# Two attention blocks on one core: B's transposed x in 512-token loads, x first on the queues, q and k weights read 128 wide, B's blocks further forward

## Chip, cores, metric

One core of a Trainium2 chip. The metric is device microseconds of one execution, median of several. The profiled span is about 1.8 us below the reported time of the same execution. In the profile's lines PE is TensorE, PEld its weight loads, DVE VectorE, ACT ScalarE, POOL GpSimd and SP SyncE; SPq and ACTq are the queues from which SyncE and ScalarE issue loads. A timeline's line gives the start, the length, the engine and what it does; a bracket is idle time before it and what ended that.

## The reference

Two independent attention blocks on 2048 tokens with 448 channels and 16 heads of 28; their outputs stand side by side.

```python
def _A_ref(x, wq, wk, wv, wo):            # full attention, one k/v head for all 16 q heads
    q = (x @ wq).reshape(B, S, H, Dh) ...  ; k = x @ wk ; v = x @ wv
    p = softmax(einsum(q, k) * Dh ** -0.5) ; o = einsum(p, v)
    return o ... @ wo
def _B_ref(x, wqkv, wo):                  # each token looks at 8 tokens, 2 apart, with 16 k/v heads
    qkv = (x @ wqkv) ...                   # idx = pos - 2 * arange(8), masked below 0
    attn = softmax(where(mask, einsum(q, kg) * scale, -1e9)) ; o = einsum(attn, vg)
    return o ... @ wo
return concatenate([a, b], axis=-1)
```

A needs 16 x 2048 x 2048 exponentials. These are 1024 blocks of 128 x 512.

## The kernel before

The kernel holds a small planner. Each operation has a guessed duration, a rank (`pr`, lower goes first) and an earliest time (`rel`); the planner simulates the engines and fixes each engine's order. On the chip the order is never changed: an engine whose next instruction has to wait stands still, and so does everything behind it.

The exponentials: scores of 3 and 2 blocks in turn go to PSUM, and ScalarE takes 3 or 2 of them in one ACTIVATE. In four rounds of each quad (64 blocks) but the first, VectorE takes one block of the three.

```python
OFF_AT = {q: (0, 2, 5, 7) for q in range(1, 16)}
OFF_AT.update({q: (0, 1, 3, 4, 6, 7, 9, 10) for q in ()})
```

The loads. `xst` is the first quarter of A's x, which TensorE transposes; the rest of x comes by transposing DMA.

```python
a("act", 0.5, ... g.xst <- A_x[0, 0:512] ..., W=["xst"], dsem="i_xa0", land=3.2, pr=-21)
a("act", 1.1, wload(g.wk, ...), W=["wk"], dsem="i_wk", land=3, pr=-20, ninc=2)
a("sp", 1.1, wload(g.wq, g.A_wq, 0, KC), ..., dsem="i_wq0", land=3, pr=-25, ninc=2)
a("gp", 1.5, wload(g.wq, g.A_wq, KC, D), ..., dsem="i_wq", land=4, pr=-7.5, ninc=2)
for c in range(1, NCH):                    # A's second to fourth quarter, 4 x 128 channels each
    for t in range(4):
        a("sp", 1.25, ... transpose=True, W=[("xT", c, t)], land=4.6, pr=-20 + c)
for t in range(4):                         # B's x, all 2048 tokens, 4 x 128 channels
    a("sp", 3.5, ... transpose=True, W=[("xT_B", t)], land=8, pr=0, rel=4)
# [...] wqkv on SP; wqv on GpSimd; output weights, then the zero rows ahead of V, on SP
```

B's q and k, and the ranks of A's v:

```python
g.bank(u.bank, p1=KC), g.wqkv[:, kt, w * D + KC * t:w * D + KC * t + KC],   # KC = 112
pr = c + (0.9 if c else 1.3)               # a_v: v of chunk c, just ahead of k of chunk c + 1
B0 = 30.0                                  # B's first block is planned from here on
```

## Time and profile before

| | before |
|---|---|
| time, median of 3 | 463.41 us (463.3 to 463.55) |
| profiled span | 461.54 us |
| ScalarE busy | 447.3 us (97%) |
| first exponential starts | 10.94 us |
| last exponential starts | 453.95 us |
| waits between exponentials over the floor | 8.84 us |

Recorded ScalarE instructions overlap by about 0.1 us, so a wait shorter than that leaves no idle time. I took the starts of ScalarE's instructions from the trace. By the median, the next one starts 0.904 us behind a 1024-wide ACTIVATE (0.903 at best), 1.330 us behind a 1536-wide one, and 0.306 and 0.054 us behind e_t and gcol, two small helpers on ScalarE. With these the 410 exponentials need 434.17 us from the first start to the last. This sum is called the floor; what the stretch takes beyond it are waits. A wait is given at the start of the ACTIVATE in front of it: the 0.87 us at 23.7 us is the one that ends with the start at 25.49, where the page has 0.65 us of idle time.

### The profile page before, as it was taken

The numbers are of one execution on the slowest core, as the hardware profiler recorded it, in microseconds if no ns is written. First come the engines' busy times: TensorE is split into PE (matmuls) and PEld (weight loads), VectorE is DVE, ScalarE is ACT, GpSimd is POOL, SyncE is SP. The second block draws the span as 40 slices with busy tenths as digits, with TensorE's granted clock in tenths as the row PEclk, the third lists the DMA queues.
The fourth block names the chain that finished last, engine by engine and source line by source line (L and its number), as shares of the span: only waits on it lengthen the run. The fifth ranks groups of instructions, "written<-read, shape, count | busy, mean of one in ns | idle before, by whom it ended". The sixth has DMA issues, their size and how long they took to land.

```text
span 461.5 us, 8681 instructions
## 1 busy us (share of the span) xinstructions
PE 422.8 (92%) x3649; PEld 168.2 (36%) x3701; DVE 365.9 (79%) x607; ACT 447.3 (97%) x430; POOL 9.3 (2%) x28
## 2 busy tenths in 40 slices
PE   7889998999998999999989999999899998997995
PEld 2332332333542434334432443334343442443331
DVE  6447888989899796888888688898889878687853
ACT  3999999999999999999999999999999999999994
POOL 7000000000000000000000000000000000000000
PEclk9999999999999999999999999999999999999999
DMA  8991121000401220002201230002200330410001
GB/s 150 164 229 33 48 75 60 11 0 22 161 21 53 89 74 27 1 14 87 91 11 50 81 101 11 12 0 92 86 26 20 111 101 12 136 46 0 11 3 48
DMA packets 41718, 27.34 MB, mean 59 GB/s; under 512 B 17090, under 2 KB 41520, under 8 KB 41680
## 3 DMA queue, kind: packets, MB, share of 16 engines
q1 hardware_dynamic: 40080, 25.35, 19.5%
q0 software_dynamic: 304, 0.73, 0.9%
q10 hardware_dynamic: 1296, 0.71, 0.5%
q8 instruction: 29, 0.48, 0.4%
q14 instruction: 9, 0.07, 0.0%
HBM read 17.60 MB, written 5.52 MB: 50 GB/s over the span
## 4 chain that ended last, share of the span: by engine, by line
ACT 88%; PE 8%; DVE 1%; DMA 1%; issue 0%; ACTq 0%
ACT expT L800 88%; PE ps L783 2%; PE ps L832 1%; PE ps L958 1%; DMA wk<-in_A_wk_dram 1%; PE ps L973 1%; PE ps L781 1%; PE ps L733 1%; PE ps L1059 1%; ACT e_t L1034 0%; PE ps L662 0%; PE ps L917 0%; DVE kT L679 0%; PE ps L747 0%; DVE PV_T L893 0%
## 5 line engine op out<-in xcount | busy, mean ns | idle before, releaser
L800 ACT ACTIVATE expT<-ps 128x1024 bf16<-128x1024 f32 (+1 forms) x410 | 441.7, 1232 | 2.8 <-PE ps L783 2.4
L783 PE MATMUL ps<-qT,kT 32*128 32x512 bf16 x833 | 123.3, 384 | 16.2 <-ACT expT L800 12.9
L832 PE MATMUL ps<-expT,v_aug 128*32 128x512 bf16 x964 | 96.1, 389 | 0.1
L864 DVE TENSOR_SCALAR d_x<-ps 128x512 f32<-128x512 f32 x60 | 41.5, 691 | 39.0 <-PE ps L783 36.8
L783 PEld LDWEIGHTS ps<-qT,kT 32*128 32x128 bf16 x833 | 30.3, 91 | 94.5 <-ACT expT L800 75.3
L781 PE MATMUL ps<-qT,kz 128*128 128x512 bf16 x160 | 50.2, 382 | 10.7 <-ACT expT L800 8.3
L832 PEld LDWEIGHTS ps<-expT,v_aug 128*32 128x32 bf16 x964 | 24.6, 93 | 60.4 <-issue 57.7
L999 DVE TENSOR_TENSOR stage<-qTB,kTB 112x1024 bf16<-112x1024 bf16 x64 | 42.2, 679 | 2.7 <-PE ps L1008 2.7
L1059 PE MATMUL ps<-ident,prod 128*112 128x128 bf16 x512 | 43.9, 225 | 0.0
L1053 DVE TENSOR_TENSOR prod<-Vsh,a_n 128x896 bf16<-128x896 bf16 x64 | 37.8, 616 | 7.2 <-PE ps L1059 7.2
L958 PE MATMUL ps<-xT_B,wqkv 128*112 128x512 bf16 x128 | 40.5, 398 | 0.1
L1059 PEld LDWEIGHTS ps<-ident,prod 128*112 128x112 bf16 x512 | 34.4, 129 | 16.8 <-issue 14.1
L874 DVE SCALAR_TENSOR_TENSOR d_u<-d_u,d_x 128x1024 f32<-128x1024 f32 x30 | 36.4, 1215 | 0.0
L876 DVE SCALAR_TENSOR_TENSOR dexp<-d_u,d_x 128x1024 int16<-128x1024 f32 x30 | 36.4, 1214 | 0.0
L872 DVE SCALAR_TENSOR_TENSOR d_u<-d_x 128x1024 f32<-128x1024 uint16 x30 | 36.3, 1210 | 0.1
L1008 PEld LDWEIGHTS ps<-ones,stage 112*128 112x128 bf16 x512 | 19.4, 96 | 8.4 <-issue 3.2
L1008 PE MATMUL ps<-ones,stage 112*128 112x4 bf16 x512 | 22.1, 167 | 0.0
L781 PEld LDWEIGHTS ps<-qT,kz 128*128 128x128 bf16 x191 | 11.9, 97 | 25.2 <-ACT expT L800 23.1
L958 PEld LDWEIGHTS ps<-xT_B,wqkv 128*112 128x112 bf16 x128 | 14.1, 128 | 16.4 <-issue 11.1
L733 PE MATMUL ps<-xT_A,wq 128*128 128x512 bf16 x57 | 18.3, 383 | 0.6 <-issue 0.3
L1066 PE MATMUL ps<-wo_B,oT 112*128 112x448 bf16 x64 | 18.1, 356 | 0.2 <-DVE oT L1062 0.2
L408 PE MATMUL ps<-warm 128*128 128x512 bf16 x54 | 17.8, 384 | 0.2 <-issue 0.2
(102 smaller groups left out, 302.9 us busy)
## 6 DMA issues: line engine op xcount, KB each, us to landing
Vsh<-v_scratch SPq DMA_DIRECT2D x16, 896.0 KB, 4.7
v_scratch<-Vst SPq DMA_DIRECT2D x16, 112.0 KB, 1.7
out_dram<-outB SPq DMA_DIRECT2D x16, 112.0 KB, 1.7
out_dram<-outA SPq DMA_DIRECT2D x14, 112.0 KB, 1.7
wqkv<-in_B_wqkv_dram SPq DMA_DIRECT2D x1, 672.0 KB, 4.7
stage<-in_A_x_dram ACTq DMA_DIRECT2D x1, 448.0 KB, 4.4
wo_B<-in_B_wo_dram SPq DMA_DIRECT2D x4, 98.0 KB
wo<-in_A_wo_dram SPq DMA_DIRECT2D x4, 98.0 KB
```

The source lines that it names most:

```text
L781: r = e.matmul(g.bank(b0 + i), g.kz[:, j, 128 * tb:128 * tb + 128], g.qT[:, sc % 2, t, :], start=True, stop=True)
L783: r = e.matmul(g.bank(b0 + i), g.kT[32 * j:32 * j + 32, 128 * tb:128 * tb + 128], g.qT[32 * j:32 * j + 32, sc % 2, t, :], start=True, stop ...
L800: x = a("act", t_exp(w), lambda e, b0=b0, w=w, n=n: e.activation(g.expT[:, n % ERING, 0:w], g.ps[:, 512 * b0:512 * b0 + w], ACT.Exp, scale ...
L832: x = e.matmul(g.bank(PVBANK, p0=32 * j, p1=32 * j + 32), g.v_aug[:, w, tb, :], src, start=first, stop=last, tile_position=(0, 32 * j))
L864: o = a("dve", t_dve_ps(512), lambda e: e.tensor_scalar(out=xx[:, 512 * h:512 * h + 512], in0=g.bank(bank), scalar1=-128.0 * A2, scalar2=1 ...
L874: a("dve", t_dve_1x(1024), lambda e: e.scalar_tensor_tensor(out=v, in0=u, scalar=EQ * F * F, in1=lo, op0=ALU.add, op1=ALU.mult), R=["d_u"] ...
L876: a("dve", t_dve_1x(1024), lambda e: e.scalar_tensor_tensor(out=out, in0=v, scalar=EL / F ** 3, in1=xx, op0=ALU.mult, op1=ALU.subtract), R ...
L958: a("pe", t_mm(512), lambda e, u=u, t=t, kt=kt, w=w: e.matmul(g.bank(u.bank, p1=KC), g.wqkv[:, kt, w * D + KC * t:w * D + KC * t + KC], g. ...
L999: op = a("dve", t_dve_2x(1024), lambda e, t=t, qv=qv, kv=kv: e.tensor_tensor(out=g.prodT[0:KC, t, :, :], in0=qv, in1=kv, op=ALU.mult), R=R ...
L1008: r = e.matmul(g.bank(u.bank, 128).rearrange("p (h w) -> p h w", w=WIN)[:, 4 * t:4 * t + 4, w], g.prodT[0:KC, t, w, :], g.ones4[:, :], sta ...
L1053: a("dve", t_dve_2x(2 * D), lambda e, qr=qr, Vv=Vv, av=av: e.tensor_tensor(out=g.prod2[:, 2 * qr:2 * qr + 2, :].rearrange("p w (d h) -> p ...
L1059: a("pe", 0.056, lambda e, u=u, t=t, w=w: e.matmul(g.bank(u.bank, 128, 128 * t, p1=KC), g.prod2[:, w, KC * t:KC * t + KC], g.ident[:, :], ...
```

## The change

Its stated intent: load B's transposed x 512 tokens at a time behind A's, so that B can begin earlier; leave the first x alone on the queues, so that the first exponential comes earlier; read B's q and k weights 128 wide; move B's blocks forward. It also changes rules of the planner and ranks. The core of the diff:

```diff
-        a("act", 1.1, wload(g.wk, g.A_wk, 0, DH), W=["wk"], dsem="i_wk", land=3, pr=-20, ninc=2)
-        a("sp", 1.1, wload(g.wq, g.A_wq, 0, KC), R=[...], W=[("wq", 0)], dsem="i_wq0", land=3, pr=-25, ninc=2)
+        a("sp", 1.1, wload(g.wk, g.A_wk, 0, DH), W=["wk"], dsem="i_wk", land=3, pr=-25, ninc=2)
+        a("act", 1.1, wload(g.wq, g.A_wq, 0, KC), R=[...], W=[("wq", 0)], dsem="i_wq0", land=3.2, pr=-20, ninc=2)
-                a("sp", 1.25, ... transpose=True)), W=[("xT", c, t)], land=4.6, pr=-20 + c)
-        for t in range(4):
-            a("sp", 3.5, ... g.xT_B[:, t, :] ..., W=[("xT_B", t)], land=8, pr=0, rel=4)
+                a("sp", 1.05, ... transpose=True)), R=["xst"], W=[("xT", c, t)], land=3.8, pr=-20 + c)
+        for c in range(NCH):
+            for t in range(4):
+                a("sp", 1.05, ... g.xT_B[:, t, 512 * c:512 * c + 512] ..., W=[("xT_B", c, t)], land=4.5, pr=-16 + c)
+        # wqkv: pr=1 -> -16.5, and 16 more columns, set to zero
-        pr = c + (0.9 if c else 1.3)
+        pr = c + 1.3
-                pr, rel = (-9.5, 0) if t == 0 else (4.0 + 10 * t, 17.0)
+                pr, rel = (-9.5, 0) if t == 0 else (3.8 + 25 * (t - 1), 17.0)
-    B0 = 30.0
+    B0 = 22.0
-                        g.bank(u.bank, p1=KC), g.wqkv[:, kt, w * D + KC * t:w * D + KC * t + KC],
+                        g.bank(u.bank), g.wqkv[:, kt, w * D + KC * t:w * D + KC * t + 128],
@@ planner: when VectorE may begin something long, and when TensorE may take a filler matmul
-                r1 = min((r for (r, o) in cand["dve"] if o.ring), default=None)
-                if r1 is not None:
-                    n = sum(1 for (_, o) in cand["act"] if o.ring)
-                    limit = max(r1, H + (0.9 if n < 1 else 0) - self.QKT - 0.2 - 0.69)
+                for (r, o) in cand["dve"]:
+                    if o.ring:
+                        end = o.sib.end if o.sib.start is not None else tE["act"] + o.sib.dur
+                        x = max(r, end + 0.9 - self.QKT - 0.2 - 0.69)
+                        limit = x if limit is None else min(limit, x)
@@ left out: the filler's condition (only where it ends ahead of the same limit), and bookkeeping for six offloads in a quad, which no quad uses
```

More of the change, by code (lines that the diff above doesn't have):

```diff
@@ L39 @@
 OFF_AT = {q: (0, 2, 5, 7) for q in range(1, 16)}
-OFF_AT.update({q: (0, 1, 3, 4, 6, 7, 9, 10) for q in ()})
+OFF_AT.update({q: (0, 2, 3, 5, 7, 8) for q in ()})
 LATE = 2
+PSTT = -0.5
 DR = 2
@@ L51 @@
                  "kids", "start", "end", "seq", "waits", "signal", "count", "vc", "ninc", "claims", "idx",
-                 "dense", "fill", "full", "opt", "alone", "lock", "ring", "tiled", "pv")
+                 "dense", "fill", "full", "opt", "alone", "lock", "ring", "tiled", "pv", "sib")
     def __init__(self, eng, dur, emit, pr, rel, name):
@@ L74, in __init__ @@
         self.pv = False
+        self.sib = None
         self.lock = isinstance(dur, Lock) or (eng == "gp" and emit is not None)
@@ L230, in run @@
                     nxt = r
-            if best is None and e == "pe" and self.FILL and T > 4 and (nxt is None or nxt > T + 0.12) and area(T) < self.IDLE:
+            if best is None and e == "pe" and self.FILL and T > 4 and (nxt is None or nxt > T + 0.12) and (limit is None or T + 0.22 + self.MODE <= limit + self.EPS) and area(T) < self.IDLE:
                 ok = [b for b in (PVBANK,) + XBANKS if self.bank_busy[b] is None and b not in self.claimed and self.bank_free_t[b] <= T]
@@ L472, in alloc @@
         self.stage = sb([128, 4096], BF16, "stage")
-        self.wqkv = sb([128, 4, 2 * D], BF16, "wqkv")
+        self.wqkv = sb([128, 4, 2 * D + 16], BF16, "wqkv")
         self.wqv = sb([128, 4, D], BF16, "wqv")
@@ L558, in consts @@
         a("gp", 0.1, lambda e: e.memset(g.wv[0:64, 3, :], 0.0), W=["wvz"], pr=-8.2)
-        a("gp", 0.8, lambda e: e.memset(g.wqkv[0:64, 3, :], 0.0), W=["wqkvz"], pr=-8.1)
+        a("gp", 0.8, lambda e: e.memset(g.wqkv[0:64, 3, 0:2 * D], 0.0), W=["wqkvz"], pr=-8.1)
+        a("gp", 0.1, lambda e: e.memset(g.wqkv[:, :, 2 * D:], 0.0), W=["wqkve"], pr=-8.1)
         a("gp", 0.5, lambda e: e.memset(g.wqv[0:64, 3, :], 0.0), W=["wqvz"], pr=-8.1)
@@ L592, in loads @@
           W=["xst"], dsem="i_xa0", land=3.2, pr=-21)
-        a("act", 1.1, wload(g.wk, g.A_wk, 0, DH), W=["wk"], dsem="i_wk", land=3, pr=-20, ninc=2)
-        a("sp", 1.1, wload(g.wq, g.A_wq, 0, KC), R=[("d_x", 0, 0), ("d_x", 0, 1)], W=[("wq", 0)], dsem="i_wq0", land=3, pr=-25, ninc=2)
+        a("sp", 1.1, wload(g.wk, g.A_wk, 0, DH), W=["wk"], dsem="i_wk", land=3, pr=-25, ninc=2)
+        a("act", 1.1, wload(g.wq, g.A_wq, 0, KC), R=[("d_x", 0, 0), ("d_x", 0, 1)], W=[("wq", 0)], dsem="i_wq0", land=3.2, pr=-20, ninc=2)
         a("gp", 1.5, wload(g.wv, g.A_wv, 0, DH), W=["wv"], dsem="i_wv", land=4, pr=-8.3, ninc=2)
@@ L598, in loads @@
             for t in range(4):
-                a("sp", 1.25, one(lambda e, c=c, t=t: e.dma_start(
+                a("sp", 1.05, one(lambda e, c=c, t=t: e.dma_start(
                     out=g.xT_A[:, t, 512 * c:512 * c + 512], in_=g.A_x[0, 512 * c:512 * c + 512, XB0[t]:XB0[t] + 128],
-                    transpose=True)), W=[("xT", c, t)], dsem=f"i_xa{c}.{t}", land=4.6, pr=-20 + c)
-        for t in range(4):
-            a("sp", 3.5, one(lambda e, t=t: e.dma_start(
-                out=g.xT_B[:, t, :], in_=g.B_x[0, :, XB0[t]:XB0[t] + 128], transpose=True)),
-              W=[("xT_B", t)], dsem=f"i_xb{t}", land=8, pr=0, rel=4)
+                    transpose=True)), R=["xst"], W=[("xT", c, t)], dsem=f"i_xa{c}.{t}", land=3.8, pr=-20 + c)
+        for c in range(NCH):
+            for t in range(4):
+                a("sp", 1.05, one(lambda e, c=c, t=t: e.dma_start(
+                    out=g.xT_B[:, t, 512 * c:512 * c + 512], in_=g.B_x[0, 512 * c:512 * c + 512, XB0[t]:XB0[t] + 128],
+                    transpose=True)), W=[("xT_B", c, t)], dsem=f"i_xb{c}.{t}", land=4.5, pr=-16 + c)
         a("sp", 1.2, lambda e: [
-            e.dma_start(out=g.wqkv[:, 0:3, :], in_=g.B_wqkv[0:384, 0:2 * D].rearrange("(t p) c -> p t c", p=128)),
-            e.dma_start(out=g.wqkv[64:128, 3, :], in_=g.B_wqkv[384:448, 0:2 * D]),
-            ], W=["wqkv"], dsem="i_wb", land=8, pr=1, rel=4, ninc=2)
+            e.dma_start(out=g.wqkv[:, 0:3, 0:2 * D], in_=g.B_wqkv[0:384, 0:2 * D].rearrange("(t p) c -> p t c", p=128)),
+            e.dma_start(out=g.wqkv[64:128, 3, 0:2 * D], in_=g.B_wqkv[384:448, 0:2 * D]),
+            ], W=["wqkv"], dsem="i_wb", land=8, pr=-16.5, rel=4, ninc=2)
         a("gp", 1.5, lambda e: [
@@ L761, in a_loop @@
         dqs = {k: [[] for _ in range(4)] for k in quads}
-        pair, late = [], []
+        pair, late, rest = [], [], {}
         g.nd = 0
+        g.nq, g.npv = {}, {}
         g.quad = None
@@ L807, in a_loop @@
             if off:
-                pair.append((us[na],) + g.d_exp(b0 + na, slot) + (1,))
+                pair.append((us[na],) + g.d_exp(b0 + na, slot, x) + (1,))
                 if len(pair) == 2:
@@ L813, in a_loop @@
                 for x in late.pop(0)[1]:
-                    dqs[x[0][:2]][x[0][3]].append(x)
-                    if all(dqs[x[0][:2]]):
-                        g.pv_group([y.pop(0) for y in dqs[x[0][:2]]])
+                    qd = x[0][:2]
+                    g.nq[qd] = g.nq.get(qd, 0) + 1
+                    n_off = len(OFF_AT[4 * qd[0] + qd[1]])
+                    if g.nq[qd] > n_off // 4 * 4:
+                        rest.setdefault(qd, []).append(x)
+                        if g.nq[qd] == n_off:
+                            g.pv_group(rest[qd])
+                        continue
+                    dqs[qd][x[0][3]].append(x)
+                    if all(dqs[qd]):
+                        g.pv_group([y.pop(0) for y in dqs[qd]])
             for u in us:
@@ L820, in a_loop @@
                     g.pv_group([x.pop(0) for x in js])
+                if u[2:] == (15, 3):
+                    left = [x.pop(0) for x in js if x]
+                    if left:
+                        g.pv_group(left)
     def pv_group(self, grp):
@@ L828, in pv @@
         def pv(e):
-            order = [o.seq for o in all_pv]
-            first, last = box[0].seq == min(order), box[0].seq == max(order)
             for (_, _, tb, j), _, src, w in grp:
+                order = [o.seq for o, js in all_pv if j in js]
+                first, last = box[0].seq == min(order), box[0].seq == max(order)
                 x = e.matmul(g.bank(PVBANK, p0=32 * j, p1=32 * j + 32), g.v_aug[:, w, tb, :], src,
@@ L841, in pv_group @@
         o.deps.update(g.evacs)
-        all_pv.append(o)
-        if len(all_pv) == 16:
+        all_pv.append((o, {y[0][3] for y in grp}))
+        g.npv[qd] = g.npv.get(qd, 0) + len(grp)
+        if g.npv[qd] == 64:
             g.a_quad_end(*qd)
@@ L853, in offload, with d_exp @@
         return int(n // 2 - g.round in OFF_AT.get(4 * us[0][0] + us[0][1], ()))
-    def d_exp(self, bank, slot):
+    def d_exp(self, bank, slot, sib):
         g, a = self, self.s.add
@@ L867, in d_exp @@
         o.ring = True
+        o.sib = sib
         if h:
@@ L872, in d_exp @@
             a("dve", t_dve_1x(1024), lambda e: e.scalar_tensor_tensor(
-                out=u, in0=lo, scalar=EP * F, in1=lo, op0=ALU.add, op1=ALU.mult), R=di, W=["d_u"], pr=-0.5)
+                out=u, in0=lo, scalar=EP * F, in1=lo, op0=ALU.add, op1=ALU.mult), R=di, W=["d_u"], pr=PSTT)
             a("dve", t_dve_1x(1024), lambda e: e.scalar_tensor_tensor(
-                out=v, in0=u, scalar=EQ * F * F, in1=lo, op0=ALU.add, op1=ALU.mult), R=["d_u"] + di, W=["d_u"], pr=-0.5)
+                out=v, in0=u, scalar=EQ * F * F, in1=lo, op0=ALU.add, op1=ALU.mult), R=["d_u"] + di, W=["d_u"], pr=PSTT)
             a("dve", t_dve_1x(1024), lambda e: e.scalar_tensor_tensor(
                 out=out, in0=v, scalar=EL / F ** 3, in1=xx, op0=ALU.mult, op1=ALU.subtract),
-              R=["d_u"] + di, W=[("dexp", m % DR)], pr=-0.5)
+              R=["d_u"] + di, W=[("dexp", m % DR)], pr=PSTT)
         return ("dexp", m % DR), out[:, 512 * h:512 * h + 512].bitcast(BF16)
@@ L894, in a_quad_end @@
                   W=kk("PV"), pr=-30)
-            o.deps.update(g.pvs[sc, t])
+            o.deps.update(x for x, _ in g.pvs[sc, t])
             evacs.append(o)
@@ L958, in b_qk @@
                     a("pe", t_mm(512), lambda e, u=u, t=t, kt=kt, w=w: e.matmul(
-                        g.bank(u.bank, p1=KC), g.wqkv[:, kt, w * D + KC * t:w * D + KC * t + KC],
+                        g.bank(u.bank), g.wqkv[:, kt, w * D + KC * t:w * D + KC * t + 128],
                         g.xT_B[:, kt, 512 * c:512 * c + 512], start=kt == 0, stop=kt == 3),
-                      R=[("xT_B", kt), "wqkv", "wqkvz"], W=[u], use=u, pr=pr, rel=rel, dense=512)
+                      R=[("xT_B", c, kt), "wqkv", "wqkvz", "wqkve"], W=[u], use=u, pr=pr, rel=rel, dense=512)
                 dst = g.kTB[:, t, PAD + 512 * c:PAD + 512 * c + 512] if w else g.qTB[:, c % 2, t, :]
@@ L975, in b_v @@
                 start=kt == 0, stop=kt == 3),
-              R=[("xT_B", kt), "wqv", "wqvz"], W=[u], use=u, pr=pr, rel=rel, dense=448)
+              R=[("xT_B", k // 4, kt), "wqv", "wqvz"], W=[u], use=u, pr=pr, rel=rel, dense=448)
         a("dve", t_dve_ps(D), lambda e, u=u: e.tensor_copy(
```

## The prediction

> **What bounds the kernel now.** I first read the page's busy shares, then the chain that ended last, then ScalarE's groups by form, then ScalarE's waits, and last the timeline of the two ends.
>
> ```profile
> PE 422.8 (92%) x3649; PEld 168.2 (36%) x3701; DVE 365.9 (79%) x607; ACT 447.3 (97%) x430; POOL 9.3 (2%) x28
> ...
> ACT 88%; PE 8%; DVE 1%; DMA 1%; issue 0%; ACTq 0%
> ```
>
> ScalarE (ACT) is busy for 447.3 of 461.5 us and carries 88% of the chain that ended last. TensorE's 92% is not the bound: a part of it is matmuls on the constant tile that only keep the engine busy. The same by form, for ScalarE alone (shape out<-in, count | busy us, mean ns | idle before):
>
> ```profile
> L800 ACT ACTIVATE expT<-ps 128x1024 bf16<-128x1024 f32 x264 | 267.9, 1084 | 0.3 <-PE ps L781 0.2
> L800 ACT ACTIVATE expT<-ps 128x1536 bf16<-128x1536 f32 x145 | 218.3, 1506 | 2.5 <-PE ps L783 2.4
> ```
>
> The means overlap (one starts before the other has drained), so they can't be added. From the starts in the trace, the next ACTIVATE starts at best 0.903 us after a 1024-wide one and 1.330 us after a 1536-wide one. 264 x 0.903 + 145 x 1.330 = 431.2 us; the eight e_t (0.306 each) and four gcol (0.054 each) make it 433.9. The timeline shows where the stream starts and where the last work lies:
>
> ```profile
> 10.94 6.07 ACT L800 ACTIVATE expT<-ps 128x1536 bf16<-128x1536 f32 x5 [1.74 <-PE ps L783]
> ...
> 25.49 3.71 ACT L800 ACTIVATE expT<-ps 128x1536 bf16<-128x1536 f32 x3 [0.65 <-PE ps L783]
> ...
> 451.61 2.94 ACT L800 ACTIVATE expT<-ps 128x1024 bf16<-128x1024 f32 x3
> ```
>
> So the span splits into 10.94 us of head, 443.6 us of exponentials (10.94 to 454.55) and 6.95 us of tail. In the middle, 443.6 - 433.9 = 9.7 us are lost to short waits. The page shows only about 1 us of them as idle, since the recorded busy times overlap and fill such gaps. One is 0.87 us, at 23.7 us, where the third chunk of k comes late; the rest are mostly 0.05 to 0.35 us each, and 2.0 us of them (18 cases) follow a matmul on wqkv. The reported 463.41 us is 1.9 us above the profiled span.
>
> **What the Trainium skill says.** Four places. "ScalarE: Activation LUTs", What ACT_TABLE_LOAD costs, gives 0.833 ns per element for every function; the trace agrees, (1330 - 903) / 512 = 0.834. So this stream gets shorter only with fewer elements. "DMA: Bandwidth & Descriptors", Issuing engines are not separate DMA queues: SP's, ACT's and GpSimd's transfers share the same 16 engines and interleave. The trace agrees: x's load took 4.4 us (issue to landing) beside two weight loads, and the transposing loads issued at 8.44 and 9.74 us took 6.8 and 6.3 us beside GpSimd's loads, where quiet ones took about 4. "TensorE: Matmul & The Clock Gate", Weight-path perf modes: fast weight load is on when there are 128 weights. The trace agrees: loads of 112 columns took 129 ns (median), loads of 128 columns 97. "Advanced Engine Details and Errata", X-Bar Transpose, calls transposing DMAs as fast as ordinary ones; here the 512-token ones are paced by their issue instead, 12 in 15.58 us, 128 KB in each 1.30 us.
>
> **The change part by part.**
>
> *Exponentials.* OFF_AT gives the same four offloads in each of 15 quads; the new six-offload list is for no quad. So the count stays at 264 + 145 + 1 and the floor stays 433.9. Nothing here can save more than the head, the tail and the 9.7 us. The new grouping of leftovers in the PV products does nothing when there are four.
>
> *First x alone.* Before, x lands at 5.19 us, wq's first part at 5.45, wk only at 6.41. VectorE waits for wk in front of the two copies of transposed x:
>
> ```profile
> 6.43 0.28 DVE L623 COPY wk<-wk 128x448 bf16<-128x448 bf16 x1 [0.66 <-DMA wk<-in_A_wk_dram]
> 6.62 0.75 DVE L656 COPY xT_A<-ps 128x512 bf16<-128x512 bf16 x2
> ```
>
> After, wk is first on SP, and I put its landing near 4 us (SP's first load landed at 4.01). x has the engines nearly alone: estimate 4.9. wq follows x on ACT's queue and lands at about 5.5, as now. The odd copies of x can then go at 5.6 instead of 6.62, but the q matmuls still need wq's copy and then nine steps of the same length. Estimate: first exponential at 10.3, a gain of 0.6 us.
>
> *The price of it.* The twelve transposing loads of A start when x has landed, at 4.9 instead of 1.94 us. At 1.30 us each the second chunk is issued by 10.1 us instead of 7.10, and the fourth by 20.5 instead of 17.52. The diff's own plan has 1.05 us each; no row of before shows such a one (1.25 to 1.27 us of issue, busy queue or not), so I count 1.30. The second chunk then lands in the stretch where GpSimd's wq and wqv loads slow everything: the load issued at 8.44 landed at 15.25. So the last quarter of that chunk may land at 13 to 15 us, where the plan implies about 12.5. Before, from the chunk's last k matmul (12.76) to finished kT (16.53) took 3.8 us. That gives kT at 16.7 to 18.9. The seventh exponential, the first that needs it, started at 17.86 before and could start at 17.2 with the earlier head (it needs kT 0.45 us ahead). Stall: 0 to 2 us, I take 1.
>
> *Third chunk.* The v matmuls now rank behind the next chunk of k. It lands at about 18.5 to 19.5, and is needed near 25. The 0.87 us stall at 23.7 should mostly go: -0.7.
>
> *B's x in sixteen loads.* 16 x 1.30 = 20.8 us of SP's queue in place of four that took 10.2 (17.56 to 27.74). But the first 512 tokens are complete at 20.5 + 1.1 (wqkv) + 4 x 1.30 + 4 to 4.5 = 31 us, and B's first q/k matmul, at 41.75 now, can move up by about 10 us; its blocks are planned 8 us earlier. This is off the bound. What it costs is a risk: TensorE's order is fixed, and a matmul that waits for a load holds up the scores behind it. I take +0.5.
>
> *wqkv 128 wide.* The matmuls still follow each other at 216 ns (median), and a score matmul follows at 312 ns after wqkv and after wq alike. The load is 32 ns shorter, mostly hidden: some tenths of 1 us over 128 loads.
>
> *VectorE's and the filler's limits in the order.* They are there to let fewer short waits arise. Of 8.8 us of short waits beside the 0.87, I take 1 us as gained, with the wider wqkv.
>
> Sum: -0.6 + 1.0 - 0.7 + 0.5 - 1.0 = -0.8 us; I add another -0.6 us for the chance that the loads keep the diff's pace. 463.4 - 1.4 = 462.0 us.
>
> **The rivals.** (1) *The late chunk dominates*: the second chunk of A's x lands at 15 us or later, TensorE stands in front of it, scores behind it are held too, and B's first matmul repeats this near 30 us. Cost 2 to 4 us, 465 to 467. For it: the 1.30 us issues, the slow landings at 15 us. Against it: the plan contains the wait for x, so the order was made knowing it. (2) *The loads keep the plan's pace*: no stall at the second chunk, the third's goes, short waits shrink by 2 us: 459 to 460. For it: the diff changes both its issue time and its landing time, as one does after a measurement. Against it: identical instructions took 1.26 us throughout. (3) *Everything is hidden*: B was never on the path, the head stays paced by x and wq: 463. (4) *TensorE or VectorE become the bound by denser work in the first 100 us* (VectorE is at 43 of 50 us there): each offloaded score waits for VectorE, so its bank comes late. A microsecond or two at most, since B's total is unchanged.
>
> **Range and chances.** The possible gain is bounded: 2% is 9.3 us, nearly all the short waits, so faster by over 2% gets 0.02. A loss of 9.3 us would need several stalls of rival 1 in a row: 0.03. Rivals 1 and 2 set the range, 459.0 to 465.5.
>
> **What would show it.** The first exponential at about 10.3 us; if it stays at 10.9, x alone brought nothing. The issues of A's transposes from about 4.9 us, 1.30 apart; if 1.05, rival 2. The idle before the exponentials between 13 and 20 us: 0 to 2 us, with TensorE waiting for a load of xT_A. No gap at 23.7. B's first wqkv matmul between 30 and 35 us. Spacing of starts summed over the exponentials: 443.6 now, 442 to 444 expected. The tail near 7 us. The prediction is wrong if the short waits change by several microseconds in either direction, which nothing in this profile lets me work out, or if a fixed-order wait for B's loads repeats for later chunks.

## The result, and the profile after

The changed kernel takes 462.02 us (median of 4, 461.78 to 462.24); the kernel before took 463.36 beside it (463.26 to 463.55). The ratio is 0.9971, 95% interval 0.9953 to 0.9988. A ratio is the mean time of one kernel's fast runs over that of the other's in the same rounds, so it isn't quite the ratio of the medians. Executions over 1.5% slower than the fastest of the same kernel are left out of the means. By its interval it is a small gain, 1.3 us.

The page of the changed kernel, busy shares and the chain that ended last:

```profile
PE 431.4 (94%) x3709; PEld 164.9 (36%) x3709; DVE 369.4 (80%) x607; ACT 446.6 (97%) x430; POOL 9.4 (2%) x29
...
ACT 87%; PE 10%; DMA 1%; DVE 1%; issue 0%
```

ScalarE is still the bound, and its busy time fell by only 0.7 us. ScalarE's groups by form in the changed kernel:

```profile
L806 ACT ACTIVATE expT<-ps 128x1024 bf16<-128x1024 f32 x264 | 265.5, 1071 | 0.2
L806 ACT ACTIVATE expT<-ps 128x1536 bf16<-128x1536 f32 x145 | 216.3, 1492 | 1.9 <-PE ps L789 1.9
```

The counts are the same, as predicted, and the idle time is down from 2.8 to 2.1 us. ScalarE's timeline around the start:

```profile
11.38 5.97 ACT L806 ACTIVATE expT<-ps 128x1536 bf16<-128x1536 f32 x5 [1.90 <-PE ps L789]
17.23 0.19 ACT L713 ACTIVATE gcol<-ps 128x4 f32<-128x4 f32 x1
17.28 7.83 ACT L806 ACTIVATE expT<-ps 128x1024 bf16<-128x1024 f32 x7
24.93 0.25 ACT L713 ACTIVATE gcol<-ps 128x4 f32<-128x4 f32 x1
24.98 6.06 ACT L806 ACTIVATE expT<-ps 128x1536 bf16<-128x1536 f32 x5
```

Two things are to be seen. The stream begins at 11.38 us, later than before (10.94), not earlier. And no bracket stands behind the later lines: the 0.65 us gap that the kernel before had at 25.49 is gone. From the starts in the trace:

| us | before | after | difference |
|---|---|---|---|
| first exponential starts | 10.94 | 11.38 | +0.44 |
| from there to the start of the last one | 443.01 | 441.46 | -1.55 |
| last start to end of span | 7.59 | 7.62 | +0.03 |
| span | 461.54 | 460.46 | -1.08 |

Why is the head no shorter? SyncE's timeline in the changed kernel:

```profile
0.80 0.46 SPq L592 DMA_DIRECT2D wk<-in_A_wk_dram  x1
1.32 0.58 SPq L593 DMA_DIRECT2D wk<-in_A_wk_dram  x1
1.94 3.86 SPq L608 DMA_TRANSPOSE xT_B<-in_B_x_dram  x3
5.84 16.33 SPq L603 DMA_TRANSPOSE xT_A<-in_A_x_dram  x12
22.21 0.58 SPq L612 DMA_DIRECT2D wqkv<-in_B_wqkv_dram  x1
```

x is not alone. A's loads have to wait for x, B's haven't, so the planner filled SP's queue with three of B's loads. x still landed 0.3 us sooner (4.87), wk 1.3 us sooner (5.08), but wq's first part, now behind x, at 6.36 instead of 5.45. And TensorE met x before its clock was up:

```profile
4.92 1.89 PE L654 MATMUL ps<-ident,stage 128*128 128x128 bf16 x16 [0.50 <-DMA stage<-in_A_x_dram]
6.60 0.89 PE L667 MATMUL ps<-xT_A,wk 128*128 128x512 bf16 x2
```

The sixteen transposes took 1.89 us, against 1.07 before. Their starts are 107 ns apart here and 56 before; in this execution the clock records show the full clock from 7.19 us on, in the profile of before from 4.56. The Trainium skill, "TensorE: Matmul & The Clock Gate", What's actually happening, says that the clock is judged over free-running windows of 3.4 us, so the moment differs between executions. The runs agree: in the 13 profiles that reached the full clock it came between 4.15 and 7.19 us.

### The profile page after: what moved, and what is told of

Its sections match the earlier page's. It is cut to its first block, busy times and chain, and to the rows that moved or that the text cites. A ratio compares the mean times of both kernels' runs of the same rounds, so it can differ in the third digit from the quotient of the medians.

```text
span 460.5 us, 8769 instructions
## 1 busy us (share of the span) xinstructions
PE 431.4 (94%) x3709; PEld 164.9 (36%) x3709; DVE 369.4 (80%) x607; ACT 446.6 (97%) x430; POOL 9.4 (2%) x29
## 4 chain that ended last, share of the span: by engine, by line
ACT 87%; PE 10%; DMA 1%; DVE 1%; issue 0%
ACT expT L806 86%; PE ps L789 2%; PE ps L850 2%; PE ps L1079 1%; PE ps L787 1%; DMA stage<-in_A_x_dram 1%; PE ps L978 1%; PE ps L738 1%; PE ps L1028 1%; ACT e_t L1054 1%; PE ps L654 0%; PE ps L937 0%; PE ps L1086 0%; PE ps L434 0%; PE ps L993 0%
## 5 line engine op out<-in xcount | busy, mean ns | idle before, releaser
L789 PE MATMUL ps<-qT,kT 32*128 32x512 bf16 x844 | 125.0, 384 | 12.4 <-ACT expT L806 10.7
L850 PE MATMUL ps<-expT,v_aug 128*32 128x512 bf16 x964 | 95.0, 389 | 0.0
L787 PE MATMUL ps<-qT,kz 128*128 128x512 bf16 x180 | 54.0, 382 | 5.6 <-ACT expT L806 4.5
L978 PE MATMUL ps<-xT_B,wqkv 128*128 128x512 bf16 x128 | 39.9, 383 | 0.0
L411 PE MATMUL ps<-warm 128*128 128x512 bf16 x65 | 21.5, 383 | 0.0
L913 DVE STREAM_TRANSPOSE PV_T<-ps 128x512 f32<-128x512 f32 (+1 forms) x17 | 11.4, 676 | 11.4 <-PE ps L850 11.3
L738 PE MATMUL ps<-xT_A,wq 128*128 128x512 bf16 x64 | 19.4, 383 | 0.0
L993 PE MATMUL ps<-wqv,xT_B 128*128 128x448 bf16 x64 | 18.4, 356 | 0.0
```

The source lines that it names most:

```text
L787: r = e.matmul(g.bank(b0 + i), g.kz[:, j, 128 * tb:128 * tb + 128], g.qT[:, sc % 2, t, :], start=True, stop=True)
L789: r = e.matmul(g.bank(b0 + i), g.kT[32 * j:32 * j + 32, 128 * tb:128 * tb + 128], g.qT[32 * j:32 * j + 32, sc % 2, t, :], start=True, stop ...
L850: x = e.matmul(g.bank(PVBANK, p0=32 * j, p1=32 * j + 32), g.v_aug[:, w, tb, :], src, start=first, stop=last, tile_position=(0, 32 * j))
L978: a("pe", t_mm(512), lambda e, u=u, t=t, kt=kt, w=w: e.matmul(g.bank(u.bank), g.wqkv[:, kt, w * D + KC * t:w * D + KC * t + 128], g.xT_B[: ...
```

## Experiments

Twelve runs were made, four to a chip. The numbers in the text are medians; "waits" are ScalarE's waits between exponentials over the floor of 434.17 us. Several kernels, the one before among them, have executions some 1.4 us or more longer than their others; where a row has such, I name both levels.

**The changed kernel again (after_again).** No edit.

> The changed kernel once more, as the yardstick of this chip. Theory: the start of the first exponential depends on when the TensorE clock is released, which differs between executions: 11.4 us when the release comes at 7.2 us, as in its first profile, and about 10.5 us when it comes before x lands. Rival: the late first exponential is fixed by the order of the loads, and stays at 11.4 us whatever the clock. Time: 0.997 of the kernel before.

461.90 us (461.79 to 462.12, six runs), ratio 0.9947 (0.9931 to 0.9962); the kernel before spread from 462.98 to 465.20 beside it, in two levels. The clock was released at 4.87 us and the first exponential started at 10.94, in line with the theory, though I had expected 10.5. From there to the last one it took 441.45 us, after 441.46 in the first profile, waits 7.28 after 7.29. So the middle repeats to 0.01 us in this pair, and in the pair of the kernel before (443.01 and 443.02). That holds for ordinary executions only: where a load lands late the middle moves too, as below. In this pair the head is what varies.

**128 against 112 columns (w112).**

```diff
-  g.bank(u.bank), g.wqkv[:, kt, w * D + KC * t:w * D + KC * t + 128],
+  g.bank(u.bank, p1=KC), g.wqkv[:, kt, w * D + KC * t:w * D + KC * t + KC],
```

> The changed kernel with wqkv read 112 columns wide again; the order of all instructions is the same. Theory (the wider weights are hidden): within 0.3 us of the changed kernel, the spacing of these matmuls stays at 216 ns. Rival (the wider weights brought the fewer short waits): 0.8 to 1.3 us slower, with about 2.0 us of waits of ScalarE right behind wqkv matmuls as in the kernel before, against 0.8 in the changed one.

463.18 us, 1.28 slower than the changed kernel beside it. The middle took 442.57 us, waits 8.40: 1.12 us more, with the order of all instructions the same. The rival has it in time, if not in place: counted from the trace, about 1.5 us of waits lie right behind a wqkv matmul, where it expected 2.0. Comparing the two kernels exponential by exponential, the delay grows only where wqkv matmuls run (37.9 to 298 us), mostly in steps of 15 to 70 ns, and stays at 1.115 us from there on. The tile's view of xT_B, in the changed kernel and then in the 112-wide one (min/median/max ns):

```profile
L978 PEld LDWEIGHTS ps<-xT_B,wqkv x128: 95/97/99, 38.1 to 296.7; 128*128 128x128 bf16 x128
L978 PE MATMUL ps<-xT_B,wqkv x128: 376/379/391, 38.1 to 296.9; 128*128 128x512 bf16 x128
```

```profile
L978 PEld LDWEIGHTS ps<-xT_B,wqkv x128: 126/129/141, 37.9 to 297.6; 128*112 128x112 bf16 x128
L978 PE MATMUL ps<-xT_B,wqkv x128: 379/379/423, 37.9 to 297.8; 128*112 128x512 bf16 x128
```

The median matmul is the same; the maximum isn't, 423 against 391. The spacing tells it: from one wqkv matmul to the next the median is 216 ns in both, but the mean is 237 against 223 (57 cases), and from a wqkv matmul to a score matmul 334 against 324 (59 cases). So most spacings are as before and some are longer. That the longer load itself makes these longer is my reading; the edit also narrows the output to 112 partitions, and no run separates the two.

**x really alone (x_alone).**

```diff
-  transpose=True)), W=[("xT_B", c, t)], ...
+  transpose=True)), R=["xst"], W=[("xT_B", c, t)], ...
```

> The changed kernel with B's transposing loads waiting for x too, so that x really is alone (in the changed kernel three of B's loads go out ahead of it). TensorE's, VectorE's and ScalarE's orders are the same. Theory (x's load takes its time alone as well): x lands within 0.2 us of 4.9, A's loads start at 4.9 instead of 5.84, the second chunk of k is ready about 0.9 us earlier, which nothing waits for: time within 0.3 us of the changed kernel. Rival (B's loads slow x): x lands at 4.4 or earlier, and the first exponential and the time gain 0.4 us or more.

465.63 us, from 463.38 to 470.83 (the last counts as slow; the five others, up to 468.41, have a ratio of 1.0020, interval 0.9986 to 1.0054). x landed at 4.82 us, so x takes its time alone as well, and that half of the theory holds. But wq's first part now landed at 5.49 instead of 6.38, and the first exponential started at 10.65 although the clock came only at 5.63: the best head of all profiles. The time was lost elsewhere, which neither theory had; the profile is of the execution of 468.41 us. VectorE's timeline:

```profile
53.28 0.62 DVE L997 CAST Vst<-ps 128x448 bf16<-128x448 f32 x1 [2.92 <-DMA v_scratch<-Vst]
```

VectorE waits 2.92 us for the store of the zero rows ahead of V, which is last in SP's queue: issued at 49.65 instead of 45.90 us, since three loads of B no longer went out during the wait for x. TensorE stands behind VectorE, and the clock records then show half clock from 53.42 to 60.25 us. The stretches of one clock window each (us, then the busy time of PE, PEld, DVE, ACT and POOL with counts, granted clock, DMA share, GB/s):

```profile
46.59:50.00 3.41, 3.21 (x23) 0.84 (x21) 3.41 (x5) 3.41 (x5) 0.00 (x0) 1.00 0.51 133
50.00:53.42 3.42, 2.02 (x16) 0.49 (x14) 0.50 (x2) 3.28 (x4) 0.00 (x0) 1.00 0.39 108
53.42:56.83 3.41, 2.86 (x12) 0.55 (x12) 3.41 (x5) 1.19 (x2) 0.00 (x0) 0.50 0.14 36
```

TensorE was busy for 2.02 of 3.42 us, and in the next window it has half its clock. Also A's second chunk landed at 15.42 us, beside GpSimd's loads, and cost a wait of 1.18 us at 14.3. TensorE's timeline shows how:

```profile
15.46 0.39 PE L667 MATMUL ps<-xT_A,wk 128*128 128x512 bf16 x1 [1.36 <-DMA xT_A<-in_A_x_dram]
```

TensorE stood in front of the chunk's last k matmul, and the scores that come behind it in the order, which needed nothing of it, were held up.

**The planner's old rules (old_rules).** The two changed rules put back as in the kernel before (the lines of the diff above, reversed, and the filler's condition).

> The changed kernel with the old rules for VectorE's limit and the filler matmuls when the order is made. Theory (the new rules bring a part of the shorter waits): 0.5 us slower than the changed kernel, the sum of ScalarE's waits between exponentials up from 7.3 to about 8 us. Rival (the gain comes from B's place and the ranks): within 0.2 us.

462.27 us, ratio 0.9953 beside 0.9947; waits 7.27 after 7.28. The theory falls, the rules bring nothing that these runs can tell from zero.

**The kernel before again (before_again).** No edit.

> The kernel before once more, profiled on this chip, since its runs beside the last experiments spread over 2.2 us where the changed kernel's spread over 0.3. Theory: its middle is as fixed as the changed kernel's (443.0 us from the first exponential to the last), and the spread lies in the head: TensorE's clock release, found between 4.6 and 7.2 us, moves the first exponential from 10.94 to about 11.5 us or later. Rival: the spread lies in the middle, in the waits between exponentials, as the late loads of x's second and third chunk move.

Its four runs lay between 463.16 and 463.25, its profile repeats the first one (443.02 us from first to last exponential, waits 8.85, the same wait of 0.87 us). So the middle of its ordinary executions is fixed, as the theory says. The other half of the theory has no support here: the clock came 0.94 us later than in the first profile, and the first exponential started at 10.82 us, 0.12 earlier. The longer executions, at 464.4 to 465.2, never fell into a profile; where they lose the time stays open.

**128 columns alone, on the kernel before (bef_w128).**

```diff
-  g.bank(u.bank, p1=KC), g.wqkv[:, kt, w * D + KC * t:w * D + KC * t + KC],
+  g.bank(u.bank), g.wqkv[:, kt, w * D + KC * t:w * D + KC * t + 128],
   # and the 16 columns of zeros behind wqkv
```

> The kernel before with one part of the change alone: wqkv read 128 columns wide. Theory (from the 112-wide run: the wider weights save 1.1 us of ScalarE's waits behind wqkv matmuls): 1.0 to 1.2 us faster than the kernel before, its stretch of exponentials 441.9 us instead of 443.0, so the wider weights alone give most of what the whole change gives. Rival (the gain needs the new order): 0.3 us or less.

Three of its six runs took 462.20 to 462.40 us, three 463.45 to 464.12; the kernel before had its levels at 463.2 to 463.6 and 464.4 to 465.0 beside it. So it is 1.0 us faster at the lower level (median 462.93, ratio 0.9982, interval 0.9962 to 1.0001, not clear by itself). The middle took 441.96 us instead of 443.02. The theory holds: this one part saves 1.06 us of the 1.55 us by which the whole change shortens the middle. Idle time on the page doesn't show it. ScalarE's waits in the kernel before, and then in this one (us in total, times, longest):

```profile
ACT expT L800 <- PE ps L783: 2.4, 2, 1.7
ACT expT L801 <- PE ps L784: 2.4, 2, 1.7
```

They read the same, 2.4 us in 2 waits, because the waits that went were hidden under the overlap.

**B later again (late_B).**

```diff
-    B0 = 22.0
+    B0 = 30.0
```

> The changed kernel with B's blocks planned from 30 us again instead of 22. Theory (B is off the path, its place only shifts where the short waits fall): within 0.5 us of the changed kernel. Rival (moving B forward brings the gain): 1 us slower, with more waits of ScalarE after 400 us, where B's work then lies.

462.64 us (462.24 to 463.10); the changed kernel had 461.90 on another chip. The middle took 442.34 us, 0.89 more than in the changed kernel. 0.37 of it is a wait at 14.5 us, since A's second chunk landed at 14.90 in this execution instead of 14.34. The remaining 0.5 us is spread, and the waits after 400 us, where the rival wanted more, are about the same (0.83 us against 0.89). So moving B forward seems worth about 0.5 us in this order, and not for the reason that the rival gives. This is one profile of a kernel whose five runs spread over 0.9 us, so the 0.5 us is not shown beyond it.

**x alone, the zero rows stored early (xa_vz).**

```diff
-  dsem="i_vz", land=2.5, pr=3, rel=4)
+  dsem="i_vz", land=2.5, pr=-16.7, rel=4)      # on top of x_alone
```

> x really alone once more, with one wait mended: the small store of the zero rows ahead of V, which VectorE waited 2.92 us for in that run, is issued ahead of B's loads. Theory (the slow run came from that store alone, and from the TensorE clock that fell to half for 6.8 us after it): the wait at 50 us is gone, no clock change in the middle, time within 0.7 us of the changed kernel, and still a wait of about 1 us at 14 us, where A's second chunk lands at 15.4. Rival (later B loads as such stall TensorE): still 2 us or more slower than the changed kernel.

Four runs of 462.08 to 463.04 us, two of 465.91 and 466.33, these with a lower mean clock (0.990 and 0.996). In the profile the wait at 50 us and the clock change are gone, so the late store is the cause of that loss in x_alone's profile. The forecast of the time failed: the median of 463.03 us is 1.1 us above the changed kernel's, not within 0.7, and the two long executions, which no profile caught, still lose some 3 us. What is left on ScalarE's timeline is the late second chunk:

```profile
16.36 1.45 ACT L806 ACTIVATE expT<-ps 128x1536 bf16<-128x1536 f32 x1 [0.80 <-PE ps L789]
```

GpSimd's part of wq landed at 13.98, VectorE waited 2.02 us for it, and the chunk landed at 15.43. The first exponential started at 10.92 us, with the clock up at 6.40.

**The old rank of v (old_vranks).**

```diff
-        pr = c + 1.3
+        pr = c + (0.9 if c else 1.3)
```

> The changed kernel with the old rank of the v matmuls, ahead of the next chunk's k matmuls. Theory (the new rank removed the wait at 23.7 us of the kernel before): a wait of 0.9 us or more is back between 20 and 30 us, since the third chunk's k again comes behind a v block, and the time goes up by 0.9 to 3 us. Rival (the wait went because the loads moved): no wait of that size, within 0.4 us of the changed kernel.

464.89 us, ratio 1.0031. On ScalarE's timeline the old wait is back, three times as long:

```profile
23.90 1.08 ACT L806 ACTIVATE expT<-ps 128x1024 bf16<-128x1024 f32 x1
27.59 4.62 ACT L806 ACTIVATE expT<-ps 128x1536 bf16<-128x1536 f32 x4 [2.61 <-PE ps L789]
```

The theory holds: with the new rank there is no such wait, with the old one there is, and with the later loads of the changed kernel it costs more. The loads do not set it in the kernel before: there the third chunk of x landed at 16.27, 15.24 and 15.09 us in three profiles (before_again and bef_w128 are the others), and the wait was 0.87 us each time. The new rank alone on the kernel before was not run.

**The old loads in the changed kernel (old_loads).** The lines of wk, wq, A's and B's x and wqkv as in the kernel before; all else as changed.

> The changed kernel with the loads of the kernel before: wq first on SP, wk on ACT, A's loads from 1.9 us on, B's x in four loads of 2048 tokens behind them. Everything else stays. Theory (the loads brought nothing: x lands at 4.7 to 5.2 us in either): within 0.4 us of the changed kernel, first exponential at about 10.9 us, but B's first wqkv matmul at about 41 us instead of 38. Rival (the new loads carry a part): 0.8 us or more slower than the changed kernel.

Four runs of 461.66 to 461.92 us, two of 463.37 and 464.32. At the lower level that is the changed kernel's time, so the new loads, a large part of the diff, bring nothing to an ordinary execution. Whether they bring steadiness is not shown: the changed kernel's ten runs all lay between 461.78 and 462.24, but on other chips, and the four of before_again, with the old loads, lay within 0.09 us. The profile here fell on a long execution (first exponential at 11.24 us, not at the expected 10.9) and shows one such loss:

```profile
18.07:21.49 3.42, 3.16 (x28) 0.99 (x28) 0.47 (x3) 3.42 (x4) 0.00 (x0) 1.00 0.91 147
21.49:24.90 3.41, 2.04 (x22) 0.75 (x24) 2.29 (x6) 3.41 (x5) 0.20 (x1) 1.00 1.06 211
24.90:28.31 3.41, 3.08 (x19) 0.59 (x17) 1.11 (x5) 2.61 (x3) 0.00 (x0) 0.50 0.95 180
```

TensorE waits for the third chunk of k, is busy for only 2.04 us of a window, has half the clock in the next, and ScalarE loses 1.37 us at 26.5. A window that happens to cover such a weak spot would explain why only some executions are long, but this is argued from one profile: xa_vz had a window busy for only 2.31 of 3.41 us at 13.23 and x_alone one of 2.05 at 12.46, and both kept the full clock. The long executions of xa_vz and of x_alone also have a lower mean clock. Most long ones of the kernel before don't (1.0), so this is not shown for it.

**Three loads mended (t1).**

```diff
+  # on top of xa_vz: GpSimd's wq early; its wqv only when A's second chunk has landed
-  dsem="i_wq", land=4, pr=-7.5, ninc=2)
+  dsem="i_wq", land=4, pr=-8.22, ninc=2)
-  W=["wqv"], dsem="i_wbv", land=5, pr=-7, ninc=2)
+  R=[("xT", 1, 3)], W=["wqv"], dsem="i_wbv", land=5, pr=-7, ninc=2)
   # VectorE's copies of wq's later parts not before 10.6 us in the plan
```

> The changed kernel with three loads mended: B's loads wait for x, the zero rows ahead of V are stored early, and GpSimd's wq goes out early and its wqv only when A's second chunk has landed. Theory (beside x, wq's first part sets the head, and GpSimd's loads hold up A's second chunk): wq lands at 5.5 instead of 6.4, the first exponential comes at 10.4 to 10.7, the second chunk by 13.5, no wait at 14 us: 0.3 to 0.5 us faster than the changed kernel. Rival (GpSimd's early wq slows x and wq's first part in its turn): first exponential at 10.9 or later, no gain.

461.81 us, ratio 0.9964; its six runs lay within 461.80 to 461.94. wq landed at 5.55, A's second chunk at 11.54 instead of 14.0 to 14.3 (15.43 in xa_vz, on which this builds), and nothing waits at 14 us. But the first exponential started at 11.09: the clock was released at 6.58 us, the transposes were slow again, and wq's copy, behind a copy of x on VectorE, started at 6.36, as in the changed kernel (6.38). So the loads do as the theory says, and in this execution the head is paced by TensorE's slow clock, not by them. The gain of 0.3 to 0.5 us did not come; the time is level with the changed kernel's 461.9, and the six runs are closer together than its (0.14 us against 0.33).

**Fewer elements on ScalarE (t1_best).**

```diff
-OFF_AT.update({q: (0, 2, 3, 5, 7, 8) for q in ()})
+OFF_AT.update({q: (0, 2, 3, 5, 7, 8) for q in (4, 12, 15)})     # on top of t1
-    B0 = 22.0  ;  BSTEP = 23.6
+    B0 = 24.0  ;  BSTEP = 24.0
```

The quads and B's places were picked with the kernel's own planner, whose figures are no measurement.

> The same, with six exponential tiles in place of four given to VectorE in the quads 4, 12 and 15, and B's blocks from 24 us at a step of 24.0. Theory (ScalarE's element count is the bound): six fewer blocks of 512 elements are 6 x 0.427 = 2.6 us less of the stretch of exponentials, of which 2 us or more arrive: 459.5 to 460 us. Rival (VectorE is too full there and lets banks come late): the short waits grow by as much as the floor falls, no gain over the changed kernel.

458.61, 458.62 and 458.62 us, ratio 0.9895 (0.9879 to 0.9910): 3.2 us faster than t1 beside it, and faster than both kernels. 2.6 us is what the six blocks are worth at 0.427 each. The gain can't be split: B's places were moved in the same run, which alone may be worth some tenths of 1 us, and the profiled run fell into a throttled execution (494.18 us, clock 0.755) and isn't used. The rival, no gain, falls by the time.

The middle, measured from the starts in the trace (us):

| profile | clock up | first exponential | first to last start | waits |
|---|---|---|---|---|
| before | 4.56 | 10.94 | 443.01 | 8.84 |
| before again | 5.50 | 10.82 | 443.02 | 8.85 |
| before, 128 columns | 4.64 | 10.84 | 441.96 | 7.79 |
| changed | 7.19 | 11.38 | 441.46 | 7.29 |
| changed again | 4.87 | 10.94 | 441.45 | 7.28 |
| changed, 112 columns | 6.53 | 11.20 | 442.57 | 8.40 |
| changed, old rules | 7.14 | 11.38 | 441.44 | 7.27 |
| changed, B late | 4.15 | 10.93 | 442.34 | 8.17 |
| changed, old rank of v | 6.25 | 10.92 | 444.65 | 10.48 |
| three loads mended | 6.58 | 11.09 | 441.47 | 7.30 |
| x alone (468.41 us, half clock in the middle) | 5.63 | 10.65 | 446.93 | 12.76 |
| x alone, zero rows early | 6.40 | 10.92 | 442.50 | 8.33 |
| changed, old loads (a long execution) | 4.42 | 11.24 | 442.75 | 8.58 |

Six of these have the changed kernel's loads unaltered. With the full clock at 4.15 to 6.25 us the first exponential started at 10.92 to 10.94, with 6.53 at 11.20, with 7.14 and 7.19 at 11.38. So a late clock explains the 11.38 of the first profile, and without it the head is as long as before.

## Why the prediction was right, and which of its steps were not

The time, 462.02 us, lies in the range and beside the predicted 462.0. The frame held: ScalarE's stream bounds the kernel, its counts did not change, so only head, tail and short waits could move. But that it came out within 0.1 us is luck: the sum came out right by errors that cancelled. Forecast were -0.6 for the head, +1.0 for the second chunk, -0.7 for the third, +0.5 for B's loads, -1.0 for rules and weights together and -0.6 for the loads' pace; found were +0.44 (0.00 in the second profile), 0, -0.87, no wait for B's loads, about -1.1 (all from the weights) and 0.

- **"Estimate: first exponential at 10.3, a gain of 0.6 us": wrong.** It started at 11.38 and 10.94 us. The step that failed is "x has the engines nearly alone" and "wq follows x on ACT's queue and lands at about 5.5": three of B's loads went out beside x, and wq landed at 6.36. wk came at 5.08, not near 4: the 4.01 us that I read for SP's first load is the landing of the first of wq's two pieces, and wk has two as well. I read the diff's wait on A's loads and did not ask what the planner would put in its place. With B's loads held back as well, wq did land at 5.5 and the head was 10.65 us, or 10.92 with a later clock (xa_vz). TensorE's clock release, up to 0.44 us of the head, was not in the prediction at all.
- **"Stall: 0 to 2 us, I take 1": wrong in size, 0.** The parts were right: 1.30 us per load, landing of the second chunk at 14.0 us. kT was ready at 17.67, in the middle of the range that I gave. But the stream began later than I thought, so it needed it later: the seventh exponential started at 18.18, 0.90 us behind the sixth, so it did not wait. Where there was a wait, in x_alone (1.18 us) and xa_vz (0.92), the chunk landed at 15.4, and what waited was not the seventh exponential for kT (0.13 us) but the fifth, whose scores stood behind TensorE's wait for the chunk. That is rival 1's mechanism at a smaller size. An early head is not needed for it: in xa_vz the stream began at 10.92 us, in after_again at 10.94, and there the chunk landed at 14.34 and nothing waited.
- **"The 0.87 us stall at 23.7 should mostly go: -0.7": right.** It went entirely, and the run with the old rank shows that without the new rank it is there.
- **"B's first q/k matmul ... +0.5": wrong.** It started at 38.1 us, not at 30 to 35, and nothing waited: B's first 512 tokens were complete at 30.12, as worked out, but the fixed order had B's matmuls later.
- **"Some tenths of 1 us over 128 loads": wrong in size.** The wider weights save 1.06 us on the kernel before and 1.12 on the changed one. I read the median spacing, 216 ns, where the loss was in the tail: the mean was 236 in the kernel before, and 220 with the wider weights. I also had the hint in my own first part, 2.0 us of waits behind wqkv matmuls, and set it aside.
- **"VectorE's and the filler's limits ... I take 1 us": wrong by itself.** The rules are worth nothing measurable (7.27 against 7.28 us of waits). The 1 us was booked for both together, and the wider weights brought all of it.

The measured account of the middle, 1.55 us: about 1.1 from the wider weights, 0.87 from the wait that the rank of v removes. These make 2.0, so at least 0.4 us came back in other short waits, and some 0.9 if B's place gains 0.5; what brought it back stays open. The new rank of A's q matmuls was never run alone. Rival 2, that the loads keep the diff's pace, fell: they kept 1.30 us.

Two readings of the prediction need a correction. Its 9.7 us of waits contain the 0.59 us of the last ACTIVATE and 0.26 us from taking 0.903 for 0.904; 8.84 are left, and 8.0 beside the 0.87. And "only with fewer elements" is too strong: 0.903 us for 1024 elements at 0.834 ns is 0.05 us more than the elements, by my estimate from the two spacings, so fewer and wider ACTIVATEs should shorten the stream as well; no run here tries it.

## What to carry to other kernels

When an engine is 97% busy and its records overlap, measure the distance from start to start; the page's idle time showed 2.4 us of waits both with and without the 1.06 us that a single edit saved. Read the mean and the tail of a spacing, not its median, where a fixed order leaves no slack. And when a wait is put in front of one group of loads, look at what a planner or a queue moves into the gap: here wq landed at 6.36 us, and at 5.49 with the gap kept free.

## What the Trainium skill lacked or had wrong

- "TensorE: Matmul & The Clock Gate", Weight-path perf modes, states when the fast load is on but not what just missing it costs a packed stream. Here 112 columns against 128: load 129 against 97 ns, mean spacing 237 against 223 ns, and 1.1 us of ScalarE's time over 128 matmuls.
- The same page, Part 1, names an idle window as what lowers the clock. Here two windows that were far from idle, with TensorE busy for 2.04 of 3.41 us and 2.02 of 3.42 us, were followed by half clock. No limit comes out of this: windows with 2.05 of 3.41 us (x_alone, from 12.46 us) and 2.10 (old_loads, from 4.42 us) were followed by full clock.
- "Advanced Engine Details and Errata", X-Bar Transpose, calls transposing DMAs as fast as ordinary ones. Here those of 512 tokens x 128 channels went out 1.30 us apart in every kernel (median; single ones up to 2.5 us), 128 KB in each 1.30 us. Issuing one took 1.26 us, where the two pieces of wk on the same queue took 0.46 and 0.58 us. The four of 2048 tokens in the kernel before went out in 10.2 us, 512 KB in each 2.5 us, twice the rate, so splitting B's x into 512-token loads cost time on SP's queue.
- No page has what GpSimd's ordinary loads do to transposing ones beside them: A's second chunk landed at 14.0 to 15.4 us beside them and at 11.54 with them moved away.
